# Attention kernel with a static scheduler: transposing DMAs, masked K spread by DMA, full rounds of products with V, and zero-weight products in TensorE's idle stretches

## The chip, the cores and the metric

One core of one Trainium2 chip. The metric is device time in microseconds (us). "Span" is the time from the first to the last instruction of one profiled execution, 1 to 2 us below the timed figure.

## The reference

```python
def _A_ref(x, wqkv, wo):                      # linear attention, 32 heads of 16, S = 2048, D = 512
    ...                                       # q, k, v from x @ wqkv
    phi = lambda t: jnp.where(t > 0, t + 1, jnp.exp(t)) + 1e-6
    pq, pk = phi(q), phi(k)
    kv = jnp.einsum("bhsd,bhse->bhde", pk, v)
    z = jnp.einsum("bhsd->bhd", pk)
    ...                                       # o = (pq kv) / (pq z + 1e-6), then o @ wo

def _B_ref(x, wqkv, wo):                      # softmax attention, same sizes
    ...
    scores = jnp.einsum("bhqd,bhkd->bhqk", q, k) * scale
    p = _softmax(scores, axis=-1)
    o = jnp.einsum("bhqk,bhkd->bhqd", p, v)
    ...                                       # o @ wo
# result: both, side by side (2048 x 1024)
```

The softmax half sets the time: 32 heads x 16 key tiles x 4 query stretches = 2,048 blocks of 128 keys by 512 queries, each of which must be exponentiated.

## The kernel before

A list scheduler in plain Python simulates the engines at build time with a duration for each operation, picks the next operation again and again, and so fixes the order in which instructions stand on each engine. On the chip nothing is chosen any more; semaphores only make an instruction wait. Score blocks go to one of two places:

- **ScalarE**: scores land in one of two PSUM slots (of three and of two blocks); one exp reads a slot (tile PT).
- **VectorE**: scores land in one of two single banks (tile pD); L756 turns them into scaled integers (tile DI), and L872, L873 and L874 make two half-precision factors (tiles DQ, DI) from three blocks at once. Such a block needs two products with V.

```python
# scores for ScalarE: one slot, then the exp that reads it
start = max(T["pe"], t0, afree[sl] + LAT, ptfree.get((row, sl), 0.0) - 0.5)
...
sch.add("act", lambda e: e.activation(PT[:, row, c0:c0 + w], SCR[sl][:, 0:w], ACTF.Exp, scale=SC), ...)

# VectorE's chain on three blocks: each operation depends on the one before
ops = [(0.07 + w * 0.00027, lambda e: e.tensor_scalar(Q, I, 0x3FF, 0x3800, op0=ALU.bitwise_and, op1=ALU.bitwise_or), ik, qk_),
       (0.07 + w * 0.00053, lambda e: e.tensor_tensor(Qh, Ih, Qh, op=ALU.mult), ik + qk_, qk_),
       (0.07 + w * 0.00027, lambda e: e.tensor_scalar(I, I, 0xFC00, 8, op0=ALU.bitwise_and, op1=ALU.bitwise_or), ik, ik)]
...
                push("dve", t_, 1, dur, r)              # may follow its predecessor at once

# x is transposed by TensorE into PSUM and copied out (L426, L419); the same for the linear attention's output
return [("pe", 4 * n * TRB, f_pe(tr, keys_ + ["identb"])),
        (lane, 0.36 * n, f_ev(lane, copy_to(lane, ...), [], [(dname, t) for t in range(t0, t0 + n)]))]

# masked K, for later groups of heads: two GpSimd operations each (L476)
for e_ in range(2):
    st.append(("pool", 0.7, f_op("pool", lambda e, e_=e_: e.tensor_scalar(KM[:, r, e_, cs], KR[:, kr, :], PAR[:, e_:e_ + 1], None, op0=ALU.mult), ...)))

# products with V: a batch of up to 8; heads g = 0..3 use four different column groups of TensorE
while nmm < PVB and any(byg.values()):
    for g in sorted(byg, key=lambda g: -len(byg[g])):
        if byg[g] and nmm < PVB:
            bt.append(byg[g].pop(0))
            nmm += len(bt[-1][2])
```

## Time and profile before

| | before |
|---|---|
| median time | 792.8 us (3 runs, 792.2 to 793.2) |
| span of the profiled run | 791.8 us |
| busy: ScalarE / VectorE / TensorE / GpSimd | 760.0 / 723.3 / 674.2 / 45.9 us |
| mean granted clock of TensorE | 0.976 |
| blocks exponentiated by ScalarE / VectorE | 1,628 / 420 |

The page and the groups are read in the prediction below. Two more views of the kernel before are needed. The first is ScalarE's timeline at the start; its columns are start, length, engine, line, operation, tiles, count, and in brackets the idle time before it with what ended it.

```profile
9.83 9.14 ACT L816 ACTIVATE PT<-pS 128x1536 f16<-128x1536 f32 x8 [0.49 <-PE pS L670]
20.66 5.97 ACT L816 ACTIVATE PT<-pS 128x1536 f16<-128x1536 f32 x5 [1.69 <-PE pS L670]
28.75 4.62 ACT L816 ACTIVATE PT<-pS 128x1024 f16<-128x1024 f32 x4 [2.12 <-PE pS L670]
```

Twice in the first 30 us ScalarE is out of scores. The second is the table of waits (engine and line, what it waited for, us in total, times, longest).

```profile
PEld pS L670 <- ACT PT L816: 299.4, 538, 1.3
...
DVE DI L756 <- PE pD L670: 25.5, 49, 1.5
```

TensorE mostly waits for ScalarE to free a slot, as it should where ScalarE is the bound. VectorE waits 25.5 us for scores.

### The profile page before, as it was taken

The page shows a single profiled execution, that of the slowest core. Times are in us where ns is not written, and L with a number is a line of the kernel's source. Part 1 is how long each engine was busy: PE and PEld are TensorE (multiplying, and loading weights), DVE is VectorE, ACT ScalarE, POOL GpSimd, SP SyncE. Part 2 cuts the span into 40 slices and gives each one's busy share as a digit, 9 for nine tenths or more (in the row PEclk, how much of TensorE's full clock was granted, in tenths as well). Part 3 has the DMA queues.
Part 4 walks back from the last instruction along what each step waited for, and adds up shares of the span by engine and source line. Part 5 has one row for each costly group of instructions (what it writes and reads, how often), then busy time and mean ns, then how long its engine had stood idle before and what let it go on. Part 6 is the DMA issues. An engine that isn't in the chain of part 4 may idle for free.

```text
span 791.8 us, 13394 instructions
## 1 busy us (share of the span) xinstructions
PE 674.2 (85%) x5585; PEld 209.6 (26%) x5634; DVE 723.3 (91%) x1264; ACT 760.0 (96%) x706; POOL 45.9 (6%) x43
## 2 busy tenths in 40 slices
PE   7889999898988888988888788988877888888875
PEld 4322333333322322222222222222222222222211
DVE  6999999989999999999999989999999997989992
ACT  6899999999999999999999999999999999999993
POOL 2000011300000001310000001121000000000000
PEclk9999999999999999999998999999999899999997
DMA  9201100000000000000000000000000000010000
GB/s 302 71 1 28 27 1 1 1 2 2 1 1 1 1 2 1 2 1 14 7 8 1 1 8 15 7 1 2 13 7 8 1 14 21 14 34 1 22 7 31
DMA packets 13139, 13.51 MB, mean 17 GB/s; under 512 B 1808, under 2 KB 12560, under 8 KB 13072
## 3 DMA queue, kind: packets, MB, share of 16 engines
q1 hardware_dynamic: 12272, 12.19, 4.8%
q8 instruction: 46, 0.75, 0.4%
q10 hardware_dynamic: 800, 0.39, 0.2%
q14 instruction: 21, 0.17, 0.1%
HBM read 8.39 MB, written 4.19 MB: 16 GB/s over the span
## 4 chain that ended last, share of the span: by engine, by line
ACT 72%; DVE 15%; PE 12%; issue 1%; POOL 0%; ACTq 0%; POOLq 0%
ACT PT L816 70%; PE pPV L935 5%; DVE DI L756 4%; PE pS L670 4%; DVE DQ L873 2%; DVE DQ L872 1%; ACT EA L534 1%; DVE DI L874 1%; PE pD L619 1%; PE pD L450 1%; DVE QMX L461 1%; DVE KMX L478 0%; DVE PQT L537 0%; DVE OT L962 0%; DVE KR L474 0%
## 5 line engine op out<-in xcount | busy, mean ns | idle before, releaser
L816 ACT ACTIVATE PT<-pS 128x1536 f16<-128x1536 f32 (+1 forms) x651 | 750.9, 1380 | 13.6 <-PE pS L670 6.5
L670 PE MATMUL pS<-QT,KM 32*128 32x512 bf16 x1628 | 256.2, 391 | 83.9 <-ACT PT L816 79.4
L756 DVE TENSOR_SCALAR DI<-pD 128x512 int16<-128x512 f32 x414 | 281.0, 689 | 29.3 <-PE pD L670 25.5
L935 PE MATMUL pPV<-PT,VV 128*17 128x512 f16 x1628 | 225.6, 390 | 1.4 <-ACT PT L816 1.0
L670 PE MATMUL pD<-QT,KM 32*128 32x512 bf16 x420 | 154.3, 392 | 2.2 <-DVE DI L756 1.1
L670 PEld LDWEIGHTS pS<-QT,KM 32*128 32x128 bf16 x1628 | 61.9, 91 | 329.1 <-ACT PT L816 299.4
L873 DVE TENSOR_TENSOR DQ<-DI,DQ 128x1536 f16<-128x1536 f16 x140 | 134.0, 957 | 2.3
L935 PE MATMUL pPV<-DQ,VV 128*17 128x512 f16 x420 | 117.0, 390 | 1.3 <-DVE OT L962 1.3
L935 PE MATMUL pPV<-DI,VV 128*17 128x512 f16 x420 | 116.2, 387 | 0.0
L872 DVE TENSOR_SCALAR DQ<-DI 128x1536 int16<-128x1536 int16 x140 | 78.4, 560 | 1.6
L874 DVE TENSOR_SCALAR DI<-DI 128x1536 int16<-128x1536 int16 x140 | 77.8, 556 | 2.0 <-DVE DQ L873 0.8
L476 POOL TENSOR_SCALAR KM<-KR,PAR 128x512 bf16<-128x512 bf16 x24 | 41.1, 1725 | 489.4 <-DVE KR L474 489.4
L935 PEld LDWEIGHTS pPV<-PT,VV 128*17 128x17 bf16 x1628 | 46.2, 88 | 85.0 <-issue 70.2
L670 PEld LDWEIGHTS pD<-QT,KM 32*128 32x128 bf16 x420 | 36.2, 91 | 14.9 <-DVE DI L756 7.0
L543 PE MATMUL pD<-Wa,xTa 128*128 128x256 bf16 x256 | 38.1, 277 | 2.1 <-DVE DI L756 1.8
L450 PE MATMUL pD<-xTb,Wb 128*128 128x512 bf16 x103 | 31.5, 390 | 6.0 <-issue 2.0
L935 PEld LDWEIGHTS pPV<-DI,VV 128*17 128x17 bf16 x420 | 30.4, 92 | 21.2 <-issue 2.0
L935 PEld LDWEIGHTS pPV<-DQ,VV 128*17 128x17 bf16 x420 | 25.9, 89 | 26.1 <-issue 16.3
L534 ACT ACTIVATE EA<-pD 128x256 bf16<-128x256 f32 (+1 forms) x48 | 29.9, 622 | 0.0
L962 DVE STREAM_TRANSPOSE OT<-pPV 128x512 f32<-128x512 f32 x32 | 22.7, 709 | 7.1 <-PE pPV L935 6.9
L543 PEld LDWEIGHTS pD<-Wa,xTa 128*128 128x128 bf16 x256 | 20.6, 98 | 18.6 <-DVE DI L756 7.2
L619 PE MATMUL pD<-WOb,ON 128*128 128x512 bf16 x57 | 18.7, 440 | 5.4 <-DVE ON L973 3.7
(86 smaller groups left out, 349.1 us busy)
## 6 DMA issues: line engine op xcount, KB each, us to landing
KNa<-in_A_x_dram SPq DMA_DIRECT2D x4, 512.0 KB, 6.7
out_dram<-OB SPq DMA_DIRECT2D x16, 128.0 KB, 1.7
out_dram<-KNa SPq DMA_DIRECT2D x16, 128.0 KB, 1.7
ON<-in_B_x_dram SPq DMA_DIRECT2D x3, 512.0 KB, 7.7
Wa<-in_A_wqkv_dram SPq DMA_DIRECT2D x1, 1536.0 KB, 12.2
Wb<-in_B_wqkv_dram SPq DMA_DIRECT2D x2, 384.0 KB, 8.5
Wb<-in_B_wqkv_dram SPq DMA_DIRECT2D x1, 512.0 KB, 6.8
WOb<-in_B_wo_dram SPq DMA_DIRECT2D x1, 512.0 KB, 12.2
```

Source lines behind the costliest of these rows:

```text
L450: return e.matmul(f32v(bk), lhsT=Wb[:, cc, kind * 512 + Gp * 128:kind * 512 + Gp * 128 + 128], rhs=xTb[:, cc, sc * 512:(sc + 1) * 512], st ...
L476: st.append(("pool", 0.7, f_op("pool", lambda e, e_=e_: e.tensor_scalar(KM[:, r, e_, cs], KR[:, kr, :], PAR[:, e_:e_ + 1], None, op0=ALU.m ...
L534: ("act", 0.1 + n * 0.00085, f_ev("act", lambda e, bk: e.activation(EA[:, q, 0:n], f32v(bk)[:, c0:c0 + n], ACTF.Exp), [], [("EA", q)])),
L543: return e.matmul(f32v(bk)[:, 256 * k_:256 * k_ + 256], lhsT=xTa[:, cc, t * 128:(t + 1) * 128], rhs=Wa[:, cc, 512 + 512 * k_ + 256 * hp:51 ...
L619: return e.matmul(f32v(bk), lhsT=src, rhs=WO[:, hb, :], start=(hb == 0), stop=(hb == 3))
L670: return e.matmul(dst, lhsT=KM[32 * g:32 * g + 32, Gp % 2, e_, j * 128:(j + 1) * 128], rhs=QT[32 * g:32 * g + 32, Gp % 2, c * 512:(c + 1) ...
L756: sch.add("dve", lambda e: e.tensor_scalar(DI[:, buf, i * 512:(i + n) * 512], DB[:, bi * 512:(bi + n) * 512], ESC, EB, op0=ALU.mult, op1=A ...
L816: sch.add("act", lambda e: e.activation(PT[:, row, c0:c0 + w], SCR[sl][:, 0:w], ACTF.Exp, scale=SC), reads=skeys(sl), writes=[("PT", row, ...
L872: (0.07 + w * 0.00027, lambda e: e.tensor_scalar(Q, I, 0x3FF, 0x3800, op0=ALU.bitwise_and, op1=ALU.bitwise_or), ik, qk_),
L873: (0.07 + w * 0.00053, lambda e: e.tensor_tensor(Qh, Ih, Qh, op=ALU.mult), ik + qk_, qk_),
L874: (0.07 + w * 0.00027, lambda e: e.tensor_scalar(I, I, 0xFC00, 8, op0=ALU.bitwise_and, op1=ALU.bitwise_or), ik, ik)]
L935: sch.add("pe", lambda e, g=g, j=j, h=h, P=P, first=first, last_=last_: e.matmul(PVb[32 * g:32 * g + 17, 0:512], lhsT=VV[:, j, vcol(h):vco ...
```

## The change

The intent: take work off VectorE so that the scheduler can give it more of ScalarE's blocks, and keep TensorE's clock up. It has five parts: (1) x and the linear attention's output are transposed by DMA; (2) masked K is written by eight small DMAs into a zeroed buffer; (3) products with V are issued in full rounds of four column groups; (4) gaps of TensorE in the plan are filled with products with a zero matrix, accumulated into a bank that is open anyway, so they add nothing; (5) the model's durations are brought closer to the chip, and a dependent VectorE operation is held back by a latency so that another is put between. The diff also moves output buffers, lets score products wait for masked K by group of heads, and raises the warming products at the start from 28 to 36. The diff at its core:

```diff
+            sch.add(lane, lambda e: e.dma_start_transpose(dst[:, :, t0 * 128:(t0 + n) * 128], x[0][t0 * 128:(t0 + n) * 128, :]),
+                    writes=[(dname, t) for t in range(t0, t0 + n)], queue="sp")
...                                                   # xT_stages and otr_job (TensorE transposes, copies) removed
+        def ont_load(o2):
+            sch.add(ont_lane, lambda e: e.dma_start_transpose(ONT[:, o2, :].rearrange("p (c n) -> p c n", n=128), OA[:, o2, :]),
+                    reads=oak(o2), writes=kst(6 + o2), queue="sp")
...
-            for e_ in range(2):
-                st.append(("pool", 0.7, f_op("pool", lambda e, e_=e_: e.tensor_scalar(KM[:, r, e_, cs], KR[:, kr, :], ...
+            def spread(bk):
+                for e_ in range(2):
+                    for g in range(4):
+                        rows = slice(32 * g + 16 * e_, 32 * g + 16 * e_ + 16)
+                        sch.add(km_lanes[4 * e_ + g], lambda e, rows=rows, e_=e_: e.dma_start(KM[rows, r, e_, cs], KR[rows, kr, :]), ...
...
-                push("dve", en + LAT, 0, 0.1 + 0.55 * n, p1)
+                push("dve", en + LAT, 0, 0.085 + 0.535 * n, p1)
...                                                   # some twenty durations like this one
-                push("dve", t_, 1, dur, r)
+                push("dve", t_ + LAT, 1, dur, r)
...
+                for rounds in range(1, PVR + 1):      # best products per time, whole rounds of 0.215 us
+                    ...
+                    sc_ = n / (0.1 + 0.215 * rounds)
...
-            for i_ in range(28):
+            for i_ in range(36):                      # warming products at the start
...
+        def fill_in(st):
+            n = min(int((st - T["pe"] - FM) / 0.215), 4)      # FM = 0.15
+            u = pvu[0]
+            if n <= 0 or u >= NU or pvopen[0] is None:
+                return
+            gs = [g for g in range(4) if 0 < pv_cnt[u][g] < NT]
+            if not gs:
+                return
+            g = gs[0]
+            def f(e):
+                for i in range(n):
+                    ins = e.matmul(PVb[32 * g:32 * g + 17, 0:512], lhsT=ZW[:], rhs=xTb[:, 0, 0:512], start=False, stop=False, ...)
...
+            if eng == "pe":
+                fill_in(st)
```

The fills don't alter the plan: they stand in the program, but the scheduler's clock does not advance for them.

## The prediction

> **What bounds the kernel now.** The kernel computes 2,048 blocks of softmax scores (128 keys by 512 queries). ScalarE exponentiates most of them (L816); VectorE does the rest with integer arithmetic (L756, then L872, L873, L874 on three blocks at once). A scheduler written into the kernel fixes the order at build time. I read first the busy shares, the clock row and the chain of waits of the page.
>
> ```profile
> PE 674.2 (85%) x5585; PEld 209.6 (26%) x5634; DVE 723.3 (91%) x1264; ACT 760.0 (96%) x706; POOL 45.9 (6%) x43
> ...
> PEclk9999999999999999999998999999999899999997
> ...
> ACT 72%; DVE 15%; PE 12%; issue 1%; POOL 0%; ACTq 0%; POOLq 0%
> ```
>
> ScalarE is busy 96% and carries 72% of the chain, so the time is ScalarE's work plus the few places where it waits. VectorE at 91% is close behind: blocks can be moved to it only while it has room. Next, the groups of instructions with shapes kept apart.
>
> ```profile
> L816 ACT ACTIVATE PT<-pS 128x1536 f16<-128x1536 f32 x326 | 518.6, 1591 | 9.9 <-PE pS L670 4.4 <-PE pD L670 4.3 <-PE pD L619 0.9
> L816 ACT ACTIVATE PT<-pS 128x1024 f16<-128x1024 f32 x325 | 380.1, 1170 | 3.7 <-PE pS L670 2.1 <-PE pD L670 1.5
> L756 DVE TENSOR_SCALAR DI<-pD 128x512 int16<-128x512 f32 x408 | 273.7, 682 | 29.3 <-PE pD L670 25.5 <-PE pS L670 2.0
> L873 DVE TENSOR_TENSOR DQ<-DI,DQ 128x1536 f16<-128x1536 f16 x140 | 134.0, 957 | 2.3
> L476 POOL TENSOR_SCALAR KM<-KR,PAR 128x512 bf16<-128x512 bf16 x24 | 41.1, 1725 | 489.4 <-DVE KR L474 489.4
> L419 DVE COPY ONT<-pD 128x512 bf16<-128x512 bf16 x16 | 6.6, 415 | 1.2 <-PE pD L609 1.2
> L419 DVE COPY xTa<-pD 128x1024 bf16<-128x1024 bf16 x8 | 5.4, 680 | 0.0
> L419 DVE COPY xTb<-pD 128x1024 bf16<-128x1024 bf16 x6 | 4.1, 680 | 0.0
> ```
>
> ScalarE does 1,628 blocks (326 threes, 325 twos), VectorE 420. The means overlap (their sum exceeds the busy time), so I take the distance from start to start where the engine doesn't wait: in the timeline 1.331 us after a three, 0.904 us after a two, 0.264 and 0.477 us after an exp of the linear attention (L534, 256 and 512 wide). ScalarE's own time is then 326 x 1.331 + 325 x 0.904 + 32 x 0.264 + 16 x 0.477 = 743.7 us. Its first exp starts at 9.8 us and its last ends at 778.5; 24.9 us of the 768.7 between are waits. The tail after it is 13.3 us. Span: 9.8 + 743.7 + 24.9 + 13.3 = 791.7.
>
> Where are the waits? In the timeline, 4.1 us are two early holes, at 20.7 and 28.7 us, while VectorE works off copies of xTb and KM. The table of stretches of 2 us shows most of the others at the low points of the clock; its columns are PE, weight load, VectorE, ScalarE, GpSimd (busy us and count), granted clock, DMA.
>
> ```profile
> 252.00:254.00 2.00, 2.00 (x15) 0.61 (x16) 1.97 (x3) 2.00 (x4) 0.00 (x0) 0.50 0.00 0
> 254.00:256.00 2.00, 2.00 (x23) 0.50 (x16) 1.34 (x5) 1.05 (x2) 0.00 (x0) 0.80 0.00 0
> ...
> 632.00:634.00 2.00, 2.00 (x15) 0.31 (x12) 1.23 (x3) 0.77 (x1) 0.00 (x0) 0.58 0.00 0
> ...
> 782.00:784.00 2.00, 2.00 (x6) 0.76 (x5) 0.69 (x1) 0.00 (x0) 0.00 (x0) 0.50 0.00 0
> ```
>
> Seven times between 251 and 767 us the clock halves for 3.4 or 6.8 us, TensorE becomes the slowest engine, and ScalarE and VectorE run dry just after. Adding ScalarE's late starts at these seven gives 9.3 us. An eighth, from 780 us, slows the sixteen last output products to 0.43 us each.
>
> **What the Trainium skill says.** (1) "TensorE: Matmul & The Clock Gate", section "What's actually happening": the clock is halved after an idle window of about 3.4 us and restored after a busy one. The trace agrees on length (3.41 or 6.83 us) but not on full idleness: TensorE was busy 1.59 us of the 2 us before the drop at 251. So thin work suffices for a drop, and filling is a sound idea. (2) "DMA: Bandwidth & Descriptors", section "Latency and other measured facts": a transposing DMA moves 261 GB/s. No transposing DMA is in this trace. (3) "TensorE: Matmul & The Clock Gate", section "Part 4: PE-mode transpose": such a transpose lands in PSUM and needs a VectorE copy. It agrees: the copies are the three L419 rows above. (4) "Perfetto Trace Analysis", section "Optimizing Scalar/DVE Operations": GpSimd and VectorE share a read port. Agrees weakly: eight L872 that ran entirely beside GpSimd's L476 took 648 ns, the other undisturbed ones 552.
>
> **The change part by part.** Counts are from the two built programs; durations from before.
>
> *Transposing DMAs.* Gone from TensorE: 192 transposes, 0.057 us apart, 11 us. Gone from VectorE, by start-to-start time: 14 pair copies at 0.60, two single at 0.33, 16 ONT copies at 0.34: 8.4 + 0.7 + 5.4 = 14.5 us. Gone from ScalarE: two xTb copies in the startup (1.1 us). At the start, 512 KB at 261 GB/s is 2.0 us (estimate from the skill's page). The 256 KB loads of before landed at 4.5 us, having been issued at 0.8; at their 340 GB/s (512 KB each 1.5 us) their data took 0.75 us, so the fixed part is near 2.9 us and the transpose lands near 5.7. Before, xTb was ready at 6.7 and the first exp came 3.1 later: 8.8 now, 1.0 us earlier. One early hole should mostly go, since 4.9 us of VectorE copies leave that stretch: 2.5 of the 4.1 us.
>
> *Masked K by DMA.* 24 GpSimd operations become 96 DMAs of 16 KB on the SP queue. At about 0.5 us an issue that is 4 us a job, needed tens of us later: hidden. VectorE gains little: 20 operations of the chain L872 to L874 ran wholly beside L476, each some 0.1 us longer than elsewhere: 2 us.
>
> *The schedule itself* is where the time is. The new durations in its model are shorter, a dependent VectorE operation is held back, and room has been made. The programs show the outcome: ScalarE gets 320 threes, 319 twos and a single (1,599 blocks), VectorE 449: 29 blocks move. ScalarE's own time falls to 320 x 1.331 + 319 x 0.904 + 0.5 + 16.1 = 730.9, so -12.8 us. VectorE pays 0.60 + (0.47 + 0.87 + 0.47) / 3 = 1.20 a block, 34.8 us, less 14.5: +20.3. Against that, a VectorE operation directly behind the one it depends on starts some 0.12 us later (L872 to L873 0.59 against 0.47), and such neighbours fall from 67 to 44 (L872, L873), 34 to 19 (L873, L874) and by 66 in the other pairs I counted (at about 0.08): 2.8 + 1.7 + 5.3 = 10 us back. VectorE ends near 723 + 20 - 10 - 2 = 731 busy.
>
> *Full rounds* make products with V run four at a time in 0.215 us. TensorE only; it has 118 us idle, so by itself nothing.
>
> *Fills.* 294 zero-weight products, up to 294 x 0.215 = 63 us of TensorE, in gaps that the plan expects. If they hold the clock, up to 9.3 us of waits go. I take 6, because a static plan misses some. In the tail, none is placed in the 2.7 us between last product with V and first output product, so I take 1.3 of the 16 x 0.21 = 3.4 us there.
>
> *Sum.* First exp 8.8; own time 730.9; waits 24.9 - 6.3 - 2.5 + 4 (VectorE now tighter) = 20; tail 12.0: 771.7. The timed median lay 1.0 above the span, so **772.5 us**.
>
> **Rivals.** (a) **VectorE becomes the bound.** At a span of 772 it has some 745 us between its first work and the tail and needs about 727: 97.6%. Against: its busiest stretch of 100 us reached 97.65 before, and 25.5 us of its idle time were waits for TensorE, which clock and rounds should shrink. For: it has only two PSUM banks. At 96.5% filling it ends near 780. (b) **Fills get in the way**: TensorE runs in order, so a fill in a gap that isn't there delays the score products that feed ScalarE. With 0.1 us on each of some 150 places, half of it reaching ScalarE, +7: 780. (c) **Fills do not count as activity**: clock drops stay, +8: 780. (d) **Slow transposing DMAs**: at half that rate the first exp comes at 11 and the early holes grow: 777. (e) **All goes well**: waits 12, tail 10: 763.
>
> **Range and chances.** From (e) to somewhat beyond one rival: 764 to 782. Faster by over 2% means below 776.9. The 12.8 us are fixed by the built program, and alone give 780, so about 3 us more are needed. Chances: faster 0.74, within 2% 0.24, slower 0.02, the last if VectorE or the fills stall ScalarE for 30 us.
>
> **What would show it.** ScalarE's busy time near 746; VectorE's 727 to 735 with dependent operations no longer adjacent; first exp before 9 us; mean clock from 0.976 to above 0.99; TensorE above 90% busy; no long wait on KM. Wrong, if ScalarE's waits for score products (pS) add up to more than before, if the drops of the clock persist, or if VectorE exceeds 97% busy with ScalarE waiting behind the banks of pD.

## The result, and the profile after

| | before | after |
|---|---|---|
| median time | 793.0 us (4 runs, 792.2 to 795.0) | 765.1 us (4 runs, 763.2 to 766.5) |
| ratio to before | | 0.9643 (0.9615 to 0.9671) |
| span | 791.8 us | 764.7 us |
| first exp starts | 9.8 us | 9.9 us |
| ScalarE's own time | 743.8 us | 730.9 us |
| ScalarE's waits between first and last exp | 24.7 us | 11.6 us |
| of these near drops of the clock / in the first 100 us / elsewhere | 10.0 / 5.2 / 9.5 us | 2.5 / 1.1 / 8.0 us |
| tail after the last exp | 13.3 us | 12.1 us |

A ratio is the mean time of one kernel's fast runs over that of the other's in the same rounds, so it is not quite the ratio of the medians quoted. Own time counts each instruction at its shortest distance from start to start (1.331, 0.904, 0.477 and 0.264 us, as in the prediction); waits are what the distances exceed it by. "Near" a drop is from 0.5 us before its start to 1.8 us after its end. (The prediction's 9.3 and 24.9 us were added up by hand from the same timeline, larger pieces only for the first.)

From the page of the changed kernel, the lines that answer to those of before:

```profile
PE 687.3 (90%) x5773; PEld 205.0 (27%) x5773; DVE 722.3 (94%) x1290; ACT 743.8 (97%) x693; POOL 8.5 (1%) x27
...
PEclk9999999999999999999999999999999989999999
...
ACT 85%; DVE 9%; PE 4%; DMA 1%; issue 0%; DVEq 0%
```

ScalarE's share of the chain rises from 72 to 85%: less of the time is spent waiting for others. The clock has one low slice left. The groups, shapes apart:

```profile
L825 ACT ACTIVATE PT<-pS 128x1536 f16<-128x1536 f32 x320 | 529.5, 1655 | 2.4 <-PE pD L676 2.1
L825 ACT ACTIVATE PT<-pS 128x1024 f16<-128x1024 f32 x319 | 393.3, 1233 | 0.4 <-PE pD L676 0.4
L765 DVE TENSOR_SCALAR DI<-pD 128x512 int16<-128x512 f32 x433 | 288.9, 682 | 13.8 <-PE pD L676 12.2
L1103 PE MATMUL pPV<-xTb,ZW 128*17 128x512 bf16 x294 | 89.7, 382 | 0.0
L882 DVE TENSOR_TENSOR DQ<-DI,DQ 128x1536 f16<-128x1536 f16 x149 | 141.4, 949 | 1.5
```

ScalarE does 320 threes and 319 twos. Its idle time ahead of them has gone from 13.6 to 2.8 us. The mean of one exp has risen (1,591 to 1,655 ns): the exps overlap in this record (the two groups add up to 922.8 us, with 736.9 us busy), so a mean can grow when the next exp is ready earlier. It is not slower work: from one start to the next, the median after a three is 1.33 us in both kernels. VectorE's L765 waits 12.2 us for scores where L756 waited 25.5. L1103 are the fills.

The start of ScalarE's timeline, in place of the three pieces of before:

```profile
9.88 26.49 ACT L825 ACTIVATE PT<-pS 128x1536 f16<-128x1536 f32 x23 [0.60 <-PE pD L676]
```

The two early holes have gone: 23 pieces without idle time. But the first exp is no earlier. The timeline of TensorE before it tells why:

```profile
1.58 4.02 PE L1003 MATMUL pD<-identb 128*128 128x128 bf16 x36 [1.58 <-POOL ZMk L368]
...
6.02 1.76 PE L452 MATMUL pS<-xTb,Wb 128*128 128x512 bf16 x4 [0.42 <-DMA xTb<-in_B_x_dram]
...
7.62 1.89 PE L452 MATMUL pD<-xTb,Wb 128*128 128x512 bf16 x8
```

The first transposing DMA lands at 5.98 us, near the 5.7 predicted. The first four products then take 1.76 us, 0.42 apart, which is half speed; the record of the clock turns to full at 7.53 us. In the kernel before, the clock was full at 5.61, and the same four products, started at 6.80, stood 0.22 apart.

Half speed is not the whole of it, as the other looks with transposing DMAs show (eleven with this one; a look is the profiled execution of a run). The first of these DMAs landed between 5.83 and 6.64 us. In six looks the clock was full by the first product; there the first exp came 3.1 us after that product, the pace of before, but x had landed only at 6.1 to 6.6 us, so it came at 9.3 to 9.8. In the five with the clock still halved it came 3.4 to 5.3 us after the product, at 9.6 to 11.8 us.

### The profile page after: what moved, and what is told of

Same layout as the page of the kernel before. It is cut to its first block, busy times and chain, and to the rows that moved or that the text cites.

```text
span 764.7 us, 13897 instructions
## 1 busy us (share of the span) xinstructions
PE 687.3 (90%) x5773; PEld 205.0 (27%) x5773; DVE 722.3 (94%) x1290; ACT 743.8 (97%) x693; POOL 8.5 (1%) x27
## 4 chain that ended last, share of the span: by engine, by line
ACT 85%; DVE 9%; PE 4%; DMA 1%; issue 0%; DVEq 0%
ACT PT L825 83%; DVE DI L765 3%; ACT EA L540 2%; DVE DQ L882 2%; PE pD L625 1%; PE pS L676 1%; DVE DI L883 1%; DVE DQ L881 1%; PE pPV L953 1%; PE pD L452 1%; DMA xTb<-in_B_x_dram 1%; DVE OT L980 0%; DVE PQT L543 0%; PE pS L452 0%; DVE KM L468 0%
## 5 line engine op out<-in xcount | busy, mean ns | idle before, releaser
L825 ACT ACTIVATE PT<-pS 128x1536 f16<-128x1536 f32 (+1 forms) x640 | 736.9, 1443 | 2.8 <-PE pD L676 2.4
L765 DVE TENSOR_SCALAR DI<-pD 128x512 int16<-128x512 f32 (+1 forms) x441 | 298.6, 692 | 13.8 <-PE pD L676 12.2
L676 PE MATMUL pS<-QT,KM 32*128 32x512 bf16 x1599 | 250.2, 386 | 56.0 <-ACT PT L825 49.3
L953 PE MATMUL pPV<-PT,VV 128*17 128x512 f16 x1599 | 203.3, 384 | 2.8 <-DVE OT L980 2.6
L676 PE MATMUL pD<-QT,KM 32*128 32x512 bf16 x449 | 163.7, 386 | 1.6 <-DVE DI L765 0.8
L882 DVE TENSOR_TENSOR DQ<-DI,DQ 128x1536 f16<-128x1536 f16 x150 | 142.1, 947 | 1.5
L953 PE MATMUL pPV<-DQ,VV 128*17 128x512 f16 x449 | 103.9, 384 | 1.0 <-DVE OT L980 0.9
L953 PE MATMUL pPV<-DI,VV 128*17 128x512 f16 x449 | 103.2, 381 | 0.1
L1103 PE MATMUL pPV<-xTb,ZW 128*17 128x512 bf16 x294 | 89.7, 382 | 0.0
L881 DVE TENSOR_SCALAR DQ<-DI 128x1536 int16<-128x1536 int16 x150 | 82.5, 550 | 0.6
L1103 PEld LDWEIGHTS pPV<-xTb,ZW 128*17 128x17 bf16 x294 | 21.1, 90 | 38.3 <-issue 28.0
L549 PEld LDWEIGHTS pD<-Wa,xTa 128*128 128x128 bf16 x256 | 20.4, 97 | 18.7 <-issue 7.4
## 6 DMA issues: line engine op xcount, KB each, us to landing
WOa<-in_A_wo_dram SPq DMA_DIRECT2D x1, 512.0 KB, 10.2
```

The lines of the kernel that those rows point to most:

```text
L549: return e.matmul(f32v(bk)[:, 256 * k_:256 * k_ + 256], lhsT=xTa[:, cc, t * 128:(t + 1) * 128], rhs=Wa[:, cc, 512 + 512 * k_ + 256 * hp:51 ...
L676: return e.matmul(dst, lhsT=KM[32 * g:32 * g + 32, Gp % 2, e_, j * 128:(j + 1) * 128], rhs=QT[32 * g:32 * g + 32, Gp % 2, c * 512:(c + 1) ...
L765: sch.add("dve", lambda e: e.tensor_scalar(DI[:, buf, i * 512:(i + n) * 512], DB[:, bi * 512:(bi + n) * 512], ESC, EB, op0=ALU.mult, op1=A ...
L881: (0.06 + w * 0.00026, lambda e: e.tensor_scalar(Q, I, 0x3FF, 0x3800, op0=ALU.bitwise_and, op1=ALU.bitwise_or), ik, qk_),
L882: (0.08 + w * 0.00052, lambda e: e.tensor_tensor(Qh, Ih, Qh, op=ALU.mult), ik + qk_, qk_),
L953: sch.add("pe", lambda e, g=g, j=j, h=h, P=P, first=first, last_=last_: e.matmul(PVb[32 * g:32 * g + 17, 0:512], lhsT=VV[:, j, vcol(h):vco ...
```

## The experiments

Times on different chips differ by some tenths of a percent, so kernels are compared by their ratio to the kernel before in the same rounds; "us" differences below are differences of these ratios times 793 us. Each such difference is uncertain by some 3 to 4 us (95%, from the two intervals). The changed kernel was measured in two sessions, with ratios 0.9643 and 0.9639.

| kernel | median us | ratio to before (95%) | clock in the look | ScalarE's waits in the look |
|---|---|---|---|---|
| changed kernel | 765.1 | 0.9643 (0.9615 to 0.9671) | 0.993 | 11.6 |
| changed kernel again | 766.1 | 0.9639 (0.9612 to 0.9666) | 0.993 | 12.4 |
| without fills | 786.0 | 0.9910 (0.9873 to 0.9947) | 0.930 | 29.3 |
| before, with fills alone | 788.7 | 0.9920 (0.9892 to 0.9948) | 0.987 | 20.4 |
| model's old durations | 769.2 | 0.9690 (0.9662 to 0.9718) | 0.995 | 10.5 |
| old batches with V | 769.8 | 0.9675 (0.9643 to 0.9708) | 0.998 | 11.8 |
| no fills, old batches | 776.6 | 0.9779 (0.9744 to 0.9813) | 0.974 | 24.5 |
| masked K by GpSimd | 771.8 | 0.9725 (0.9682 to 0.9768) | 0.986 | 13.4 |
| TensorE transposes | 781.9 | 0.9856 (0.9817 to 0.9895) | 0.980 | 25.5 |
| twice the fills | 781.5 | 0.9860 (0.9823 to 0.9896) | 1.000 | 26.9 |
| fills in more places | 764.5 | 0.9630 (0.9604 to 0.9657) | 0.998 | 10.5 |
| fine fills | 764.8 | 0.9633 (0.9607 to 0.9659) | 0.998 | 10.4 |
| fine fills, longer warm-up | 764.5 | 0.9621 (0.9594 to 0.9647) | 0.996 | 11.3 |

All were correct. The theory going in was that the moved blocks and the held clock carry the gain; the rival, that removed work and the tighter order do it and the fills are decoration.

### Without fills

```diff
         def fill_in(st):
             n = min(int((st - T["pe"] - FM) / 0.215), 4)
             u = pvu[0]
+            return
```

> The changed kernel without its 294 zero-weight products; nothing else differs, the order of all other instructions is the same. Theory 1 (the fills hold the clock, and the held clock is most of the 13.2 us of ScalarE waits that went): six to eight stretches at half clock come back, mean clock near 0.975, ScalarE's waits rise from 11.6 us by 6 to 10, time 771 to 775 us. Theory 2 (rounds, order and fewer copies did it; fills are idle decoration): clock stays near 0.99 or falls without cost, time within 1.5 us of the changed kernel, 764 to 767.

Ratio 0.991, so the fills are worth 21 us, twice the most that was expected. Everything else of the change together, which takes 12.9 us off ScalarE's own time, is then worth 0.9%. From the page without fills:

```profile
PE 644.0 (82%) x5431; PEld 189.6 (24%) x5479; DVE 725.0 (93%) x1290; ACT 747.4 (96%) x693; POOL 8.5 (1%) x27
...
PEclk9989989998799999998999997999999999898977
```

Its record of the clock has twenty stretches at half speed before the end, of 3.4 to 10.2 us. Nineteen of them begin before the last exp, where the kernel before had seven. 24.4 of the 29.3 us of ScalarE's waits lie near them. The table of stretches of 2 us around one of them (columns as in the prediction):

```profile
170.00:172.00 2.00, 1.30 (x18) 0.34 (x16) 2.00 (x6) 2.00 (x4) 0.00 (x0) 1.00 0.00 0
172.00:174.00 2.00, 1.31 (x13) 0.30 (x13) 2.00 (x4) 2.00 (x3) 0.00 (x0) 1.00 0.00 0
174.00:176.00 2.00, 1.59 (x11) 0.43 (x14) 2.00 (x4) 2.00 (x3) 0.00 (x0) 0.52 0.00 0
...
178.00:180.00 2.00, 2.00 (x18) 1.13 (x16) 1.24 (x3) 1.94 (x2) 0.00 (x0) 0.50 0.00 0
180.00:182.00 2.00, 2.00 (x24) 0.54 (x23) 1.97 (x5) 1.46 (x2) 0.00 (x0) 0.78 0.01 4
```

TensorE is busy two thirds of 4 us, all others are well; then the clock halves, TensorE is busy throughout, and at 178 to 182 VectorE and ScalarE run dry. So a drop does not need an idle TensorE, and a TensorE that has become quicker at its work loses its clock more often.

### The fills alone, in the kernel before

```diff
+        ZW = sb("ZW", [128, 17], BF)           # zeroed by VectorE at the start
...
+            if eng == "pe":
+                fill_in(st)                     # as in the changed kernel
             T[eng] = st + dur
```

> The kernel before with the fills alone: 136 of them fit into its plan's gaps. Theory 1: most of the seven mid-run drops of the clock go, and up to the 9.3 us of waits tied to them: 784 to 788 us. Theory 2: within 1.5 us of before, 791 to 794. If fills get in the way: above 794.

Ratio 0.992: 6 us, in absolute time 788.7, just above what theory 1 expected, on a chip where before read 794.9. Waits near drops fell from 10.0 to 6.1 us in the look, and five short drops were left in mid-run against seven before. So the same device is worth 6 us there (136 fills) and 21 us here (294). The prediction had sized it by the first.

### The model's old durations

```diff
-                push("dve", t_ + LAT, 1, dur, r)
+                push("dve", t_, 1, dur, r)
...
-                push("dve", en + LAT, 0, 0.085 + 0.535 * n, p1)
+                push("dve", en + LAT, 0, 0.1 + 0.55 * n, p1)
...                                              # and all other durations as before
```

> The changed kernel with the durations of before in its scheduler's model and without the added delay between dependent VectorE operations. The built program gives VectorE 441 blocks instead of 449 (so ScalarE 8 more, 8 x 0.447 = 3.6 us), and dependent neighbours L872-L873 rise from 44 to 75. Theory A (the model's costs turn the room on VectorE into time): 3.6 us own time and 2 to 4 us more waits, 770 to 773 us. Theory B (the removed copies alone matter, the static order takes care of itself): at most +3.6, 765 to 769 us.

Ratio 0.969, 3.7 us slower, barely clear of the noise; the 8 blocks alone explain 3.6, and the waits in the look are not higher (10.5 us). Theory A's added waits did not come. Dependent neighbours on VectorE (75 against 44 pairs of the chain's first and second operation) cost VectorE time, which it turned out to have: 726.1 us busy.

### The old batches of products with V

```diff
-                for rounds in range(1, PVR + 1):
...
+            while nmm < PVB and any(byg.values()):      # PVB = 8, as before
```

> The changed kernel with the batches of products with V of before (up to 8, not filled to rounds of four). The built program gives VectorE 446 blocks (3 fewer, 1.3 us) and has 199 fills. Theory A (rounds concern TensorE alone, which has slack): 766 to 768 us. Theory B (ragged batches delay the score products and are much of the waits that went): ScalarE's waits rise by 5 us or more, 771 us or above.

Ratio 0.9675, 2.6 us slower by the ratios, but their intervals overlap; 1.3 of that are the three blocks. The time lies between the two forecasts. The waits in the look are the same (11.8 us), so theory B fell; besides the blocks the look has only a late first exp, at 11.8 us, with the clock full at 10.90. That the old batches cost more than their three blocks while the fills are there is not shown.

### No fills and old batches

The two edits above together.

> The changed kernel without fills and with the old batches of products with V. Without fills alone the clock fell to 0.93 with some twenty drops, far more than the nine of before. Theory C (full rounds finish sooner and leave TensorE idle longer between, so they cause these drops): with the old batches the clock is 0.96 or above, ScalarE's waits near drops fall from 24 to 8-14 us, time 775 to 782 us. Theory D (the drops come from the transposes that left TensorE and from the tighter schedule, not from the rounds): clock 0.93 to 0.94, time 785 us or more.

Ratio 0.978, which is 10 us **faster** than with full rounds and no fills. From its page:

```profile
PE 665.9 (86%) x5476; PEld 198.7 (26%) x5476; DVE 723.5 (93%) x1287; ACT 747.6 (96%) x694; POOL 8.5 (1%) x27
...
PEclk8999999999998999998999899999999999999999
```

TensorE's work is all but the same (three products with V fewer) but it is busy 22 us longer than with full rounds without fills (665.9 against 644.0), though its clock was the higher one, and higher clocks shorten work. (Up to 10 us of this may be 48 matmuls without a record in the other trace, which has 5,431 for 5,479 weight loads; at full speed they stand 0.22 us apart.) The clock is 0.974 against 0.930, and the waits near drops are 14.5 us. Theory C is borne out: ragged batches keep TensorE occupied, full rounds let it finish and fall idle, and without fills that idleness costs the clock. Full rounds cost 10 us without fills; with them, a gain beyond the three blocks is not shown.

The traces show the thin work directly. In each look the turns of the clock stand on a grid of 3.41 us. Of the grid's windows at full clock before the last exp, matmuls covered less than 70% in 38 without fills, 23 with no fills and old batches, 23 in the kernel before and 3 in the changed kernel. The drops before the last exp were 19, 9, 7 and 1.

### Masked K by GpSimd

```diff
-            st.append(("pool", 5.0, spread))
+            for e_ in range(2):
+                st.append(("pool", 0.7, f_op("pool", lambda e, e_=e_: e.tensor_scalar(KM[:, r, e_, cs], KR[:, kr, :], ...
```

> The changed kernel with the masked K made by GpSimd again instead of by DMA; blocks unchanged (449 on VectorE), 292 fills. Theory A (both ways are hidden, GpSimd disturbs VectorE by 2 us at most): 764.5 to 768 us, GpSimd busy 45 us. Theory B (VectorE is so full now that GpSimd beside it costs ScalarE waits): 769 us or more, VectorE's L881 to L883 longer in those stretches.

Ratio 0.9725, 6.8 us slower than the changed kernel on the same chip, so the number is theory B's, but its mechanism isn't shown. Operations of the chain that ran wholly, or but for a twentieth, beside GpSimd were longer (four L877 782 ns against 548, four L879 610 against 546, four L878 957 against 945), 1.2 us in all. What the look shows besides is a first exp at 11.8 us (clock full only at 10.85), a tail of 13.2 us with a drop of the clock in it, and four drops in mid-run. Against the second look of the changed kernel that is 2.2 us at the start, 2.3 in the tail and 1.0 of waits. The run with old batches, which keeps the DMAs, had the same late first exp, so part of this may be chance of the look. The clock of the four runs with GpSimd was 0.982 to 0.991 against 0.993 to 0.998 in the changed kernel. Why a plan with the same blocks and 292 fills drops more often is open; the gain of the DMA spread is therefore 1.2 us by contention and some 5 us that are not explained.

### TensorE transposes and copies again

```diff
-            sch.add(lane, lambda e: e.dma_start_transpose(dst[:, :, t0 * 128:(t0 + n) * 128], ...
+        load(ON[:, 0:2, :], xbn[:, 0:2, :], ...)          # loads, xT_stages, otr_job, 28 warming products as before
...
-                        ..., ("pool", 2.6, lambda bk: ont_load(o2))],
+        def otr_job(t, **kw):                             # four transposes into pD, copy to ONT
```

> The changed kernel with TensorE transposes and VectorE copies again for x and for the linear attention's output; everything else of the change stays. The built program gives VectorE 443 blocks (6 fewer than the changed kernel, 2.7 us of ScalarE's own time) and has 269 fills. Theory A (transposing DMAs are worth the room they make and little else): 767 to 771 us. Theory B (they are the heart of the change): 775 us or more, VectorE above 735 us busy, the early holes of ScalarE back (4 us).

Ratio 0.9856, 17 us slower: I had leaned to theory A, and it fell. VectorE's 732.1 us stay under theory B's figure, but the early holes are back, as the timeline of ScalarE shows:

```profile
9.67 11.46 ACT L841 ACTIVATE PT<-pS 128x1536 f16<-128x1536 f32 x10 [0.49 <-PE pS L692]
23.09 3.71 ACT L841 ACTIVATE PT<-pS 128x1536 f16<-128x1536 f32 x3 [1.97 <-PE pS L692]
29.74 11.40 ACT L841 ACTIVATE PT<-pS 128x1024 f16<-128x1024 f32 x10 [2.94 <-PE pD L692]
```

Set against the second run of the changed kernel, whose waits in the first 100 us, near drops and elsewhere were 1.1, 3.9 and 7.4 us, its look has 6.0, 8.9 and 10.6, and 2.6 us more own time. So, by one look of each, the transposing DMAs are worth some 5 us in the startup, 2.6 in moved blocks, 5 near drops and 3 elsewhere, rather than the room alone.

### Twice the fills in each gap

```diff
-                for i in range(n):
+                for i in range(2 * n):
                     ins = e.matmul(PVb[32 * g:32 * g + 17, 0:512], lhsT=ZW[:], rhs=xTb[:, 0, 0:512], ...
```

> The changed kernel with twice the fills in each gap (588 instead of 294, so each filled gap overflows its plan). Theory A (the planned gaps are real and no more than a fill's width is left over in them, so the extra 63 us of TensorE delay score products): TensorE above 95% busy, ScalarE's waits up by 8 us or more, 773 us or more, though the clock stays full. Theory B (TensorE has slack and ScalarE's two buffers absorb it): within 2 us of the changed kernel.

```profile
PE 731.7 (94%) x6067; PEld 226.9 (29%) x6067; DVE 725.3 (93%) x1290; ACT 750.6 (96%) x693; POOL 8.6 (1%) x27
...
PEclk9999999999999999999999999999999999999999
...
ACT 40%; PE 36%; DVE 22%; DMA 1%; issue 1%; DVEq 0%
```

Ratio 0.986, 17.5 us slower at a perfect clock. TensorE was 94% busy, one point short of what theory A said, but its share of the chain is 36%, and ScalarE's waits are 26.9 us in many pieces, none over 0.7 us and none near a drop. The 294 fills stay 0.15 us clear of the next planned product, and there the waits were 11.6 us; once the gaps overflow, the rival of the prediction is real. The margin itself was not varied.

### The changed kernel again, fills in more places, fine fills, a longer warm-up

These four shared a chip and five rounds. The cut of the fine fills is shown against the kernel with more fills, that of the longer warm-up against the fine fills.

> The changed kernel unaltered, once more, on the chip of the next three: 764 to 767 us, and a measure of how far the earlier comparisons across chips can be trusted. First exp between 9.3 and 11.8 us, as in the runs so far.

```diff
+            if not gs:                                   # no accumulation open: a free bank of pD, up to 12 in the tail
+                bk = DBANK[max(fr, key=lambda i: (dfree[i], i))]
+                ... e.matmul(bk[0][0:17, bk[2]:bk[2] + 512], lhsT=ZW[:], rhs=xTb[:, 0, 0:512], start=True, stop=True, ...)
```

> The changed kernel with fills also where no accumulation with V is open: into a free score bank, and 12 in the stretch before the last output products (310 fills in all). Theory E (the drops left, at unit boundaries and in the tail, are gaps that the fills could not reach): no drop near the end, tail 12.1 to some 10.5 us, 2 us faster, 762 to 764 us. Rival (the window is free-running, so drops fall where they will): tail and drops as before, within 1 us of the unaltered one.

```diff
-            n = min(int((st - T["pe"] - FM) / 0.215), 4 if u < NU else 12)
+            n = min(int((st - T["pe"] - FM) / 0.058), 16 if u < NU else 44)     # 128 columns each
```

> As the kernel with more fills, but each of 128 columns instead of 512, so the same margin of 0.15 us is kept and gaps under 0.365 us can be filled too (1,552 fills of about 0.058 us, 90 us instead of 67). Theory A (what hurts is overflow, not filling): clock 1.0, ScalarE's waits 9 to 11 us, 761 to 764 us. Rival (each fill costs a weight load and an issue that the gap does not hold): waits up by 4 us or more, 768 us or more.

```diff
-            for i_ in range(36):
+            for i_ in range(44):
```

> As the kernel with fine fills, with 44 instead of 36 warming products at the start, so TensorE does not pause before the first x has landed (6.0 to 6.6 us). Theory W (the pause leaves the clock halved until 7.5 to 11 us in some executions): first exp at 9.3 to 9.6 us in the look, median 0.5 to 1 us below that of the fine fills. Rival (the phase of the window decides): no difference beyond 0.5 us.

Ratios 0.9639, 0.9630, 0.9633 and 0.9621: the order is as expected but for the fine fills; the intervals overlap, so nothing beyond "no slower" is shown. The last is the fastest kernel by its mean, 1.4 us ahead of the changed kernel. In the look, waits fell from 12.4 to 10.5 and 10.4 us, and fine fills, with 1,552 weight loads, did no harm. The tail was 10.9, 10.9, 10.7 and 10.7 us; the unaltered kernel had no drop in its tail this time, so the tail's fills could not show anything. The drop at 622 us, 6.8 us long in both looks of the changed kernel, was still there with more and with fine fills, for 3.4 us. With the longer warm-up it was gone, but there was one of 6.8 us at 13.1 us. The first exp of that look came at 9.8 us although the clock was full at 6.27, because x landed at 6.64. Theory W is not confirmed.

## Why the prediction was right or wrong, point by point

The time, 765.1 us, lies inside the range of 764 to 782 and in the likelier class, but 7.4 us below the point. The misses of its four terms, +1.1, 0, -8.4 and +0.1 us, make nearly all of that; the result is near its case (e), in which all goes well. By the terms of its sum:

- **ScalarE's own time** was right: 730.9 predicted and measured. It was read from the built program's counts, and a count leaves nothing to judge.
- **First exp at 8.8** was wrong: 9.9. The step that failed is "xTb was ready at 6.7 and the first exp came 3.1 later: 8.8 now": it took over the pace of products at full clock, but TensorE ran at half speed until 7.53 us, which cost 0.7 us. The landing of the transposing DMA (5.98 against 5.7) was nearly right in this look, but later in most, and where the pace of 3.1 us held, the landing at 6.1 to 6.6 kept the first exp above 9.2. That TensorE's pause before x lands keeps the clock down is not shown: in the other looks with transposing DMAs the clock was full between 4.5 and 10.9 us, and with the old durations it was full from 4.46 through a pause of 1.4 us.
- **Waits of 20** was wrong: 11.6. Near drops 7.5 us went (6 taken, written as 6.3 in the sum), and in the first 100 us 4.1 (2.5 taken). The largest miss is "+ 4 (VectorE now tighter)": elsewhere the waits fell by 1.5. VectorE ended at 722.3 us, not 731: the 29 blocks cost it 21.8 us of busy time instead of 34.8, because its operations on average took less once dependent neighbours were separated (L873 to L882: 0.899 to 0.876 us each; L872 to L881: 0.523 to 0.497), and short operations of the linear attention and of the normalization took 6.6 us less, where "10 us back" had been taken for all of this. Rival (a) did not come: one stretch of 100 us ran at 99.4% on VectorE with ScalarE idle 0.1 us.
- **Tail of 12.0** was right by its size (12.1; 10.9 in the second run), but its mechanism, fills that hold the clock there, is not shown. In the first run a drop at 755 us slowed half of the last sixteen products, in the second none did; and without any fill the tail was 12.6 us with full rounds and 10.8 with old batches. Where a drop falls decided, so the hit is luck.
- **"If they hold the clock, up to 9.3 us of waits go"** was right for the kernel before (6 us measured) and wrong for the change. The drops to be avoided are not those of the kernel before but those that the rest of the change would have made: twenty, and 21 us. The prediction treated the parts as a sum.
- **"TensorE only; it has 118 us idle, so by itself nothing"**, said of full rounds, was right with fills (2.6 us by the ratios, within the noise, half of it three blocks) and wrong without (10 us lost). Idle time of TensorE does cost something: the clock.
- **Transposing DMAs** were undersized. Room, 1.0 and 2.5 us added up to a few us; undoing them costs 17.
- **Masked K hidden, gain of 2 us**: contention was 1.2 us, but undoing it cost 6.8; open.
- Rivals (b) and (c) did not come. Doubling the fills shows that (b) comes once the gaps overflow, and dropping them shows that (c) is false: zero weights count as activity.

What would show it: ScalarE's busy time (746 said, 743.8 found), the clock above 0.99 (0.993) and no long wait on KM held; VectorE (727 to 735) and the first exp before 9 us did not; TensorE above 90% was 89.9%.

## What to carry to other kernels

Size a measure that protects the clock against the kernel that it will be in, not against the one that you have: a saving on TensorE thins its work and can cost the clock more than it saves (full rounds without fills: 10 us), and filling its gaps then pays for both. Fill only gaps that the schedule is sure of, with a margin; here 294 products gained 21 us and 588 lost 17 against that. Where a static order is built, read the moved work from the built programs' counts: that term of a prediction comes out exactly.

## What the Trainium skill lacked or had wrong

- "TensorE: Matmul & The Clock Gate", section "What's actually happening", names an idle window as what halves the clock. Here it halved with TensorE's matmuls covering 1.30 and 1.31 us of the two stretches of 2 us before (at 174 us without fills). A later section of the page, "A second HAM failure mode: psum-queue depth-cycling", does tell of a clock that falls through short idle times. How much activity holds it is not stated. In the fourteen looks here, before the last exp, the clock fell after all nine windows of 3.41 us that matmuls covered to less than 55%, after 46 of the 718 from 55 to 85%, and after none of the 2,282 above (the ends of matmuls are modelled). Lengths of 3.41 and 6.83 us, three times 10.2, agree with the page's window.
- The same page does not say whether products with zero weights count as activity for this gate. They do: the mean clock was 0.993 with 294 of them, 1.000 with 588, and 0.930 without.
- The same page's advice is to avoid idle gaps; it does not warn that a faster TensorE phase brings drops. Full rounds without fills were 10 us slower than ragged ones (clock 0.930 against 0.974).
- "DMA: Bandwidth & Descriptors", section "Latency and other measured facts", gives 261 GB/s for a transposing DMA with a non-contiguous middle dimension and some 350 to 400 for the contiguous case; the prediction took the first and left the condition out. In eleven looks the second of two (512 KB from memory) landed 1.4 to 1.8 us after the first, which is 290 to 360 GB/s. The page gives no time to landing for such a DMA: the first landed 5.0 to 5.8 us after its issue, and the two issues together held the SP queue for 4.9 us in the look of the changed kernel. Transposes of 128 x 512 within the core's memory landed after 2.4 us.
- "Perfetto Trace Analysis", section "Optimizing Scalar/DVE Operations", warns of the port that GpSimd and VectorE share; that section gives no size (other pages of the skill treat the port at more length). Beside GpSimd the first operation of the chain took 782 ns instead of 548, the third 610 instead of 546, the second 957 instead of 945 (four cases each).
